# Last tile of a two-dimensional convolution: when its planes are built, which engine sums, and who issues its eight output writes

## The chip, the cores and the metric

The kernel runs on one core of one Trainium2 chip. The metric is the time of one execution on the device in microseconds (us); several executions were timed and the median is given. A separate execution was profiled; its trace gives the start and length of every instruction, and all times "at" some microsecond below are counted from the first instruction of that trace.

The engines go by the names of the profile: PE is TensorE (matrix products) and PEld its weight loads, DVE is VectorE, ACT is ScalarE, POOL is GpSimd, SP is SyncE, which here only issues DMAs. A small q (SPq, ACTq) means that only the sequencer of the engine is at work, as when it issues a DMA. PSUM is the memory that PE writes its products to, in eight banks; SBUF is the working memory.

## What is computed

```python
def reference(x, w):             # x: (1, 224, 224, 96) bf16, w: (7, 7, 96, 96) bf16
    wp = jnp.pad(w, ((0, H - K), (0, W - K), (0, 0), (0, 0)))
    Xf = rfft2(x.astype(f32), axes=(1, 2))
    Wf = rfft2(wp.astype(f32), axes=(0, 1))
    Yf = jnp.einsum('bhwi,hwio->bhwo', Xf, Wf)
    return irfft2(Yf, (H, W), axes=(1, 2)).astype(bf16)
```

This is a circular convolution of a 224 x 224 image of 96 channels with a 7 x 7 filter that maps 96 channels to 96.

## The kernel before

**Tiles and rounds.** The image is cut into 7 tiles of 32 columns (`t` = 0 to 6; the last is `TL`). The rows are cut into 8 blocks of 28 (`NJ` = 8, `B` = 28), and each block of rows, with its halo, is transformed along the rows into 17 points (`NS` = 17). Points 0 and 16 are real (`REAL`), the other 15 are complex. One pass over a point of a tile is a round, `b_round(t, s, ...)` at line 510. The columns are not transformed: they are convolved directly, with the even and the odd columns apart, by three sets of taps (`TAPS`, 4 + 4 + 3), and a complex product is made of three real ones (`part` 0, 1, 2).

**A round on PE.** Its stationary operands (the weights that PEld loads) are slices of 128 columns of the transformed image `xf` or of planes `J`, which are sums and differences of `xf`; its moving operand is the transformed filter `WF`, 96 columns wide. A complex round has 33 matrix products: 12 and 7 of them go to bank `b0`, the other 14 to bank `b1`. Between the two runs stands `mid()`, and after them `end()`: there other jobs are put in, in the last tile the inverse transforms of the tile before (`Gm` against `tt`, 384 columns wide).

**A round on the other engines.** ACT copies the shared products out of `b0` into `tt_` (times -0.5 where needed). DVE makes `u` from `b0` and `tt_`, with one `scalar_tensor_tensor`, and `v` from `b1` and `tt_`. Then `ysum` (line 601) adds `v` and `u` and writes bf16. POOL makes this sum, except in rounds with `ydve` true, in which DVE makes it. `tt_`, `u` and `v` have two buffers each. In a round with planes the sum on POOL waits for the last plane operation.

**Planes.** `jit(t, g)` (line 474) makes the planes of a group of three rounds (`JGB`, the last group has two: 15 and 16), with three DVE operations: all four differences in one, then a sum, then two sums. They are put in behind `v` of the first round of the group before (`plan`, line 859): in the last tile in rounds 0, 3, 6, 9 and 12. There `ydve` is true (line 876), so that in rounds 3, 6, 9 and 12 DVE makes the sum and then the planes.

**The last tile's end.** Other tiles write their results to DRAM and read them back in another order. The last one keeps them in SBUF: rounds 0 to 12 (`SA` = 13) in `YA`, rounds 13 to 16 in `YB`. DVE then turns blocks of 32 x 32: `turn_a(0)` to `turn_a(3)` make `TA` out of `YA` (in rounds 13, 14, 15 and 16), and `turn_b` makes `TB` out of `YB`, in two operations, once the sum of round 16 is there. Then come 16 output pieces `(j, h)`, `j` a block of rows and `h` half of the tile's columns. For each, `first` (line 892) makes one product of 384 columns with the matrix `GA` from `TA`; `second` (line 897) adds four products of 96 columns with `GB[b]` from `TB` in the same bank, and copies the bank into `yo`, by DVE and ACT in turn. Eight `first` are made ahead, while `TB` is awaited; each later one stands behind a `second`. `GA` and `GB` are parts of `GY`, five matrices of 112 columns.

**The writes.** After both halves of a block `j`, one DMA of 168 KB writes it to the output: SP issues `j` = 0, 2, 4, 6, POOL 1, 3, 5, and ACT 7:

```python
eng = SE if j == NJ - 1 else GE if j % 2 else DE          # line 915
eng.dma_start(out=out[0, j * B:(j + 1) * B, ...].rearrange("m (q w) c -> m q (w c)", q=4), in_=yo[0:MO, ...])
```

**Order.** Each engine runs its instructions in the order in which the program calls them (`_Ordered`, line 76); a waiting instruction holds all that stand behind it on its engine. All of them are recorded in that helper, so every line of the profile says L86, and one goes by the tiles' names.

Of the kernel before, what the change touches and what calls it, by code (L numbers as in the profile page):

```python
# [14 lines left out]
B = 28  # L15
# [19 lines left out]
SA = 13  # L35
NB4 = 4
YMAX = 3
YBUF = 4
JGB = ((0, 3), (3, 6), (6, 9), (9, 12), (12, 15), (15, 17))
LAG = 4  # L40
CQ = {2: (11, 0), 3: (11, 2), 4: (9, 5), 5: (6, 8), 6: (3, 8)}
SH2 = (0, 8, 13, 17)
MERGE = ()
NP2 = 0
WARM0 = 2
BIAS = 3000.0

# [6 lines left out]
def kernel(  # L54
# [60 lines left out]
        return r  # L115

    def evac(out_ap, in_ap, n):
        if tail[0]:
            return tail_evac(out_ap, in_ap, n)
        cv, ca = 180 + 1.0 * n, 160 + 0.85 * n  # L120
        if load["v"] + cv <= load["a"] + ca:
            load["v"] += cv
            return VE.tensor_copy(out=out_ap, in_=in_ap)
        load["a"] += ca
        return SE.copy(out=out_ap, in_=in_ap)

    def tail_evac(out_ap, in_ap, n):
        tail[0] += 1
        return VE.tensor_copy(out=out_ap, in_=in_ap) if tail[0] % 2 else SE.copy(out=out_ap, in_=in_ap)

    def dma(out_ap, in_ap):
        return DE.dma_start(out=out_ap, in_=in_ap)
# [341 lines left out]
    def jit(t, g):  # L474
# [24 lines left out]
            sub(Jb[:, 5:7, i0:i1], Jb[:, 0:4:2, i0:i1], Jb[:, 1:4:2, i0:i1], ALU.add, 2 * PP * (c1 - c0)),  # L499
        ]  # L500

    yf_cur = {}

    def pairs(ap):
# [5 lines left out]
    def b_round(t, s, mid, end, ydve=False, planes=()):  # L510
# [25 lines left out]
                TE.matmul(o, lhsT=pl[:, (HALO - k) * NJ:(HALO - k) * NJ + 128], rhs=wv,  # L536
                          start=(k == 0 and not add), stop=(k == len(tp) - 1 and not both and m != 2 or not add and not both and k == len(tp) - 1))
        b0, b1 = bank(), bank()
        merge = t < 2 and s in MERGE
        tt_ = tv_pool.tile([128, 4 * C], F32, name="tt_")  # L540
        if s in REAL:
            for part in range(2):
# [21 lines left out]
        else:  # L564
            v = tv_pool.tile([128, 2, 2, C], F32, name="v")
            if merge:
                conv(b0, 2 * C, 0, 0, both=True)
                conv(b0, 2 * C, 2, 0, add=True)
                conv(b0, 3 * C, 1, 0, add=True)
                conv(b0, 0, 0, 1)  # L570
                conv(b0, C, 0, 2)
                SE.mul(out=tt_[:], in_=b0[:, 0:4 * C], mul=-0.5)
                u, pr = tt_[:, 2 * C:4 * C].rearrange("p (m o) -> p m o", m=2), tt_[:, 0:2 * C]
            else:
                for part in range(3):
# [63 lines left out]
    xs = xf_bufs[(TL + 1) % 2].rearrange("c p r s w j -> c (p r s w j)")  # L639
    assert NA + 2 * NBL <= 4 * NS * POS * NJ and NA <= 2 * (XW + 32)  # L640
    YA = xn_all[:, 0:NA].rearrange("p (g s o) -> p g s o", s=SR, o=2)
    TA = xs[:, 0:NA].rearrange("p (g w j e) -> p w j g e", j=NJ, w=4, e=4)
    TB = xs[:, NA:NA + NBL].rearrange("p (g w j e) -> p w j g e", j=NJ, w=4, e=4)
    YB = xs[:, NA + NBL:NA + 2 * NBL].rearrange("p (g s o) -> p g s o", s=SRB, o=2)
# [16 lines left out]
    def g_parts():  # L661
        for q in range(4):
            dma(GX[q * SR:q * SR + 2 * SA, 0, q * B:q * B + B], G[0:2 * SA, 0:B])
            yield
        for q in range(4):
            for b in range(NB4):
                r = q * SR + b * SRB
                dma(GX[r:r + SRB, 1 + b, q * B:q * B + B], G[2 * SA:2 * NS, 0:B])
                yield
        for k in range(NB4 + 1):  # L670
            GE.tensor_copy(out=GY[:, k].rearrange("p (m q) -> p q m", q=4), in_=GX[:, k].rearrange("p (q m) -> p q m", q=4))
            yield

    yo_free = [J_bufs[2][0:4 * B, i * PXC * C:(i + 1) * PXC * C] for i in range(2)]
# [120 lines left out]
    for r in range(NS + LAG):  # L795
        if r == 0:
            add(0, 4, fj[1][1] + fj[2][1])
        for p in range(3):
            if r == (1, 3, 5)[p]:
                new_xf(1, SH2[p], SH2[p + 1])  # L800
                fj = f_jobs(1, p)
                if p == 2:
                    for jg in range(2):
                        fj[jg][-1] = then_load(fj[jg][-1], 2, jg)
                add(2 * r + 1, 2 * r + (5, 5, 4)[p], fj[0] + fj[1])
        for p in range(3):
            if r == SH2[p + 1] + 1 - (p == 2):
                new_xf(2, SH2[p], SH2[p + 1])
                fj = f_jobs(2, p)
                if p == 2:  # L810
                    for jg in range(2):
                        fj[jg][-1] = then_load(fj[jg][-1], 3, jg)
                add(2 * r, 2 * r + (8, 7, 5)[p], fj[0] + fj[1])
        if r == PGRP[-2][1] + 1:
            assert not any(q[2] for q in qs[:len(PGRP) - 1])
            wtmp_cm.__exit__(None, None, None)
            t_pool = ctx.enter_context(tc.tile_pool(name="tt", bufs=NTT, side="right"))
            t2_pool = ctx.enter_context(tc.tile_pool(name="tt2", bufs=1, side="right"))
            yo_pool = ctx.enter_context(tc.tile_pool(name="yo", bufs=2, side="right"))
            g_pool = ctx.enter_context(tc.tile_pool(name="gp", bufs=1, side="right"))  # L820
            GX = g_pool.tile([128, 1 + NB4, 4 * B], BF16, name="GX")
            GY = g_pool.tile([128, 1 + NB4, 4 * B], BF16, name="GY")
            GA, GB = GY[:, 0], GY[:, 1:]
            GE.memset(GX[:], 0.0)
        if r == NS + 3:
            queue_c(0)
        for t in range(2):
            s = r - LAG * t
            if not 0 <= s < NS:
                continue  # L830
# [12 lines left out]
    for t in range(2, NT):  # L843
        if t == TL:
            GE.memset(YA[:, :, 2 * SA:, :].rearrange("p g s o -> p g (s o)"), 0.0)
        else:
            scr_tiles[t] = dr_pool.tile([TW, NJ, NS, 4 * C], BF16, name="scr")
        qs = []
        if t + 1 < NT:
            add(4 if t == 2 else 0, 26, a_jobs(t + 1))  # L850
        nold, nnew = CQ[t]
        k1 = 2 * NS if t < TL else 2 * NS - 2
        k0 = 10 if t == 2 else 3
        km = k0 + -(-(k1 - k0) * nold // (nold + nnew))
        add(k0, km, cj[:nold])
        cn = c_jobs(t - 1)
        cj = cn[nnew:]
        add(km, k1, cn[:nnew])
        plan = {}
        for g, (s0, s1) in enumerate(JGB):  # L860
            if g + 1 < len(JGB) or t + 1 < NT:
                plan[s0 if g + 1 < len(JGB) else s0 - 1] = g
        for s in range(NS):
            now = ()
            if s in plan:
                g = plan[s]
# [12 lines left out]
    turn_b()  # L879
    load["v"] = 2 * BIAS + load["a"]  # L880
    for f in cj:
        f()
    tail[0] = 2
    assert not pend
    if NP2:
        for c in reversed(ps_cms):
# [3 lines left out]
    MO = 4 * B  # L890

    def first(j, h):
        pc = bank()[0:MO, 0:NC]
        TE.matmul(pc.rearrange("p (w g e) -> p w g e", w=2, e=4), lhsT=GA, rhs=TA[:, 2 * h:2 * h + 2, j], start=True, stop=False)
        return pc

    def second(j, h, pc, yo):
        po = pc.rearrange("p (w g b e) -> p b w g e", w=2, b=NB4, e=4)
        for b in range(NB4):
            TE.matmul(po[:, b], lhsT=GB[:, b], rhs=TB[:, 2 * h:2 * h + 2, j], start=False, stop=b == NB4 - 1)  # L900
        tail_evac(yo[0:MO, (j % 2) * 2 * NC + h * NC:(j % 2) * 2 * NC + (h + 1) * NC], pc, NC)
# [47 lines left out]
```

## Time and profile before

| | us |
|---|---|
| median of 3 executions | 265.87 |
| lowest, highest | 265.08, 266.1 |
| the profiled execution | 266.41 |
| its span, first to last instruction | 264.7 |
| PE busy | 252.5 (95% of the span) |
| DVE busy | 215.8 (82%) |
| ACT busy | 198.6 (75%) |
| POOL busy | 101.5 (38%) |
| mean granted TensorE clock | 0.993 |

The busy time of PE covers nearly all of the span, because a matrix product of 96 columns shows as 206 ns, while the next one starts 42 to 43 ns later: starts have to be compared, not lengths. The engines work at different things at the end of the span than in the rest of it, so that shares of the whole say little of a change to the last tile.

### The profile page before, as it was taken

To read this page: it belongs to the slowest core of one execution; us is meant where nothing else is said; L and a number is where in the kernel's file an instruction comes from. 1 tells how busy PE (TensorE), PEld (TensorE's weight loads), DVE (VectorE), ACT (ScalarE), POOL (GpSimd) and SP (SyncE) were. 2 spreads that over 40 slices of the span, in tenths; PEclk is the share of its full clock that TensorE was granted. 3 is DMA by queue.
4 is the path that set the end of the run, shared out by engine and by line. 5 is a ranking of instruction groups with operands and counts; after the bars stand their busy time and mean duration, and the time that the engine had idled before them with its cause. 6 is when DMAs were issued, how large, how long until landed. Compare 5 with 4: busy or idle time off the path is not lost.

```text
span 264.7 us, 12207 instructions
## 1 busy us (share of the span) xinstructions
PE 252.5 (95%) x5160; PEld 234.3 (89%) x5160; DVE 215.8 (82%) x459; ACT 198.6 (75%) x500; POOL 101.5 (38%) x166
## 2 busy tenths in 40 slices
PE   8799998999999999999999999999999999999981
PEld 3569898999999999998999998999999999999861
DVE  5729799898978979977888788777978889899981
ACT  5529997659795566898988869989798886666652
POOL 7781033345355553234123332543143222424420
PEclk9999999999999999999999999999999999999997
DMA  6766210451111299896979449597959753585135
GB/s 162 182 192 152 73 51 2 154 159 47 50 47 47 85 254 208 239 268 180 290 226 244 150 108 315 180 258 185 325 193 206 209 186 125 145 169 155 55 111 175
DMA packets 41416, 43.44 MB, mean 164 GB/s; under 512 B 30836, under 2 KB 33104, under 8 KB 41362
## 3 DMA queue, kind: packets, MB, share of 16 engines
q1 hardware_dynamic: 41044, 41.98, 56.6%
q8 instruction: 40, 0.66, 1.1%
q0 software_dynamic: 192, 0.52, 0.7%
q10 hardware_dynamic: 126, 0.17, 0.2%
q14 instruction: 14, 0.11, 0.1%
HBM read 22.09 MB, written 19.66 MB: 158 GB/s over the span
## 4 chain that ended last, share of the span: by engine, by line
PE 82%; ACT 5%; DVE 4%; issue 3%; DMA 3%; POOL 1%; SPq 1%; DVEq 0%; ACTq 0%
PE pb L86 82%; ACT WF L86 3%; DMA WF<-in_x_dram 3%; DVE WF L86 1%; ACT xf L86 1%; POOL yf L86 1%; DVE J L86 1%; DVE u L86 1%; DVE xf L86 1%; SPq L86 1%; DVE yf L86 0%; ACT tt L86 0%; DVE v L86 0%; ACT tt__676 L86 0%; ACT tt__2951 L86 0%
## 5 line engine op out<-in xcount | busy, mean ns | idle before, releaser
L86 PE MATMUL pb<-WF,J 96*128 96x96 bf16 x2821 | 162.6, 206 | 0.5 <-DVE WF L86 0.3
L86 PEld LDWEIGHTS <-J 96*128 96x128 bf16 x2821 | 137.9, 98 | 8.7 <-DVE u L86 1.5
L86 POOL TENSOR_TENSOR yf<-v,u 128x384 bf16<-128x384 f32 x70 | 69.1, 1001 | 129.5 <-issue 69.2
L86 ACT CAST xf<-pb 96x408 bf16<-96x408 f32 (+3 forms) x143 | 67.2, 487 | 10.3 <-PE pb L86 8.5
L86 PE MATMUL pb<-WF,xf 96*128 96x96 bf16 x952 | 60.2, 206 | 1.1 <-ACT xf L86 0.5
L86 DVE TENSOR_TENSOR J<-xf 96x1824 bf16<-96x1824 bf16 (+1 forms) x84 | 57.5, 724 | 0.1
L86 PEld LDWEIGHTS <-xf 96*128 96x128 bf16 x952 | 47.3, 98 | 1.9 <-issue 0.9
L86 PE MATMUL pb<-Fm,xn 118*128 118x136 bf16 (+3 forms) x640 | 45.5, 199 | 0.9 <-DVE u L86 0.8
L86 ACT CAST WF<-pb 96x480 bf16<-96x480 f32 (+1 forms) x59 | 29.0, 573 | 5.0 <-PE pb L86 5.0
L86 PE MATMUL pb<-tt,Gm 102*84 102x384 bf16 (+1 forms) x132 | 32.1, 326 | 0.0
L86 PEld LDWEIGHTS <-xn 118*128 118x128 bf16 x640 | 30.5, 97 | 1.2 <-issue 1.2
L86 ACT CAST yo<-pb 84x384 bf16<-84x384 f32 (+1 forms) x66 | 28.2, 484 | 2.9 <-PE pb L86 2.6
L86 ACT CAST J<-pb 84x384 bf16<-84x384 f32 (+1 forms) x65 | 28.0, 484 | 2.8 <-PE pb L86 2.8
L86 DVE TENSOR_TENSOR J<-J 96x912 bf16<-96x912 bf16 (+2 forms) x42 | 22.8, 542 | 0.0
L86 PE MATMUL pb<-wq 98*128 98x120 bf16 (+1 forms) x288 | 21.2, 225 | 0.0
L86 PEld LDWEIGHTS <-wq 98*128 98x128 bf16 x288 | 19.4, 148 | 0.2
L86 PE MATMUL pb<-wu 128*128 128x512 bf16 x43 | 11.8, 435 | 1.1 <-DVE ct L86 1.1
L86 DVE TENSOR_TENSOR yf<-v,u 128x384 bf16<-128x384 f32 x20 | 11.3, 567 | 0.7
L86 PEld LDWEIGHTS <-Gm 102*84 102x84 bf16 (+1 forms) x132 | 11.1, 117 | 0.8
L86 DVE CAST WF<-pb 96x480 bf16<-96x480 f32 (+1 forms) x13 | 7.5, 610 | 5.4 <-PE pb L86 5.2
L86 POOL TENSOR_TENSOR xn<-v,u 128x384 bf16<-128x384 f32 x8 | 7.2, 926 | 11.8 <-DVE v L86 11.8
L86 ACT COPY xf<-xf 96x816 bf16<-96x816 bf16 (+3 forms) x20 | 11.2, 621 | 0.0
(404 smaller groups left out, 254.3 us busy)
## 6 DMA issues: line engine op xcount, KB each, us to landing
scr<-yf SPq DMA_DIRECT2D x30, 288.0 KB
xn<-in_x_dram SPq DMA_DIRECT2D x12, 672.0 KB
tt<-scr SPq DMA_DIRECT2D x24, 336.0 KB
out_dram<-yo SPq DMA_DIRECT2D x12, 252.0 KB
out_dram<-J SPq DMA_DIRECT2D x12, 252.0 KB
tt<-scr SPq DMA_DIRECT2D x6, 288.0 KB
WF<-in_x_dram SPq DMA_DIRECT2D x2, 672.0 KB
scr<-yf SPq DMA_DIRECT2D x6, 192.0 KB
```

The costliest lines, as they stand in the source:

```text
L86: r = fn(*a, **k)
```

## The change

All of it concerns the last tile (`t == TL`), except that the matrices `GY` are set up with 16 further columns of zeros.

- The planes of rounds 15 and 16 are not made together in round 12 in a buffer `J`. `late_planes` makes them by themselves: those of round 16 in round 8 (one operation of 608 elements), those of round 15 in round 11 (608, 152 and 304 elements). They lie in free parts of the buffer `xf` of the other tile.
- The sums of rounds 3, 6, 9 and 12 go from DVE to POOL (`t != TL` in the last call).
- In rounds 14 and 15 the product that both halves of `u` share is written to both by PE, with a moving operand that repeats its 96 columns (192 wide, four products), and the other terms are added to it in PSUM. DVE's `u` falls away; ACT copies it out of PSUM, as a part of `tt_`, and POOL reads it there.
- `GY` has 128 columns, and `pc` all 128 rows; 112 are copied out.
- Six `first` are made ahead, not eight.
- Of the 16 copies DVE makes seven (numbers 1, 3, 5, 8, 10, 12, 14) and ACT nine, among them both of block 7.
- SP issues the writes of blocks 0, 2, 4, 5, 6, 7, POOL those of 1 and 3, ACT none.

```diff
+TAILV = (1, 3, 5, 8, 10, 12, 14)
-MERGE = ()
+MERGE = (14, 15)
+FI = 6
+LROUND = {8: 16, 11: 15}
...
     def tail_evac(out_ap, in_ap, n):
         tail[0] += 1
-        return VE.tensor_copy(out=out_ap, in_=in_ap) if tail[0] % 2 else SE.copy(out=out_ap, in_=in_ap)
+        return VE.tensor_copy(out=out_ap, in_=in_ap) if tail[0] in TAILV else SE.copy(out=out_ap, in_=in_ap)
...
+    def late_planes(s):
+        x0, x1 = (xf_tiles[TL][0:C, ph, :, s].rearrange("c r w j -> c r (w j)") for ph in range(2))
+        o = LATE[s]
+        Jb = jbuf[(TL, s)] = xs[0:C, o:o + 7 * PP].rearrange("c (k q) -> c k q", q=PP)
+        pd, rd, qd = x1.ap
+        dpl = bass.AP(x1.tensor, x1.offset - NJ, [pd, [NJ, 2], rd, qd])
+
+        def sub(o, a, b, op, n):
+            def f():
+                load["v"] += 170 + n * PP / 1.92
+                return VE.tensor_tensor(out=o, in0=a, in1=b, op=op)
+            return f
+        ops = [sub(Jb[:, 0:4].rearrange("c (k r) q -> c k r q", r=2), dpl, x0.unsqueeze(1).to_broadcast([C, 2, 2, PP]), ALU.subtract, 4)]
+        if s not in REAL:
+            ops += [sub(Jb[:, 4], x0[:, 0], x0[:, 1], ALU.add, 1), sub(Jb[:, 5:7], Jb[:, 0:4:2], Jb[:, 1:4:2], ALU.add, 2)]
+        return ops
...
-        merge = t < 2 and s in MERGE
+        merge = t == TL and s in MERGE
...
                 conv(b0, C, 0, 2)
-                SE.mul(out=tt_[:], in_=b0[:, 0:4 * C], mul=-0.5)
+                SE.mul(out=tt_[:, 2 * C:4 * C], in_=b0[:, 2 * C:4 * C], mul=-0.5)
+                SE.copy(out=tt_[:, 0:2 * C], in_=b0[:, 0:2 * C])
...
+    LATE = {NS - 2: NA * 3 // 4, NS - 1: NA + 2 * NBL}
...
-            GY = g_pool.tile([128, 1 + NB4, 4 * B], BF16, name="GY")
+            GY = g_pool.tile([128, 1 + NB4, 128], BF16, name="GY")
             GE.memset(GX[:], 0.0)
+            GE.memset(GY[:, :, 4 * B:], 0.0)
...
-            if g + 1 < len(JGB) or t + 1 < NT:
+            if g + 1 < len(JGB) - (t == TL) or t + 1 < NT:
...
+            if t == TL and s in LROUND:
+                now = late_planes(LROUND[s])
...
-            b_round(t, s, mid, fills(qs, 2 * s + 1), bool(now) and not (t == TL and s >= SA), now)
+            b_round(t, s, mid, fills(qs, 2 * s + 1), bool(now) and t != TL, now)
...
-    live = {k: first(*k) for k in order[:8]}
+    live = {k: first(*k) for k in order[:FI]}
...
-        if 8 <= k < len(order):
+        if FI <= k < len(order):
...
-            eng = SE if j == NJ - 1 else GE if j % 2 else DE
+            eng = GE if j in (1, 3) else DE
```

More of the change, by code (lines that the diff above doesn't have):

```diff
@@ L117, in evac @@
     def evac(out_ap, in_ap, n):
-        if tail[0]:
-            return tail_evac(out_ap, in_ap, n)
         cv, ca = 180 + 1.0 * n, 160 + 0.85 * n
@@ L641 @@
     YA = xn_all[:, 0:NA].rearrange("p (g s o) -> p g s o", s=SR, o=2)
+    LATE = {NS - 2: NA * 3 // 4, NS - 1: NA + 2 * NBL}
+    assert 7 * PP <= NA // 4 and NA + 2 * NBL + 7 * PP <= 4 * NS * POS * NJ
     TA = xs[:, 0:NA].rearrange("p (g w j e) -> p w j g e", j=NJ, w=4, e=4)
@@ L670, in g_parts @@
         for k in range(NB4 + 1):
-            GE.tensor_copy(out=GY[:, k].rearrange("p (m q) -> p q m", q=4), in_=GX[:, k].rearrange("p (q m) -> p q m", q=4))
+            GE.tensor_copy(out=GY[:, k, 0:4 * B].rearrange("p (m q) -> p q m", q=4), in_=GX[:, k].rearrange("p (q m) -> p q m", q=4))
             yield
@@ L882 @@
         f()
-    tail[0] = 2
+    tail[0] = 0
     assert not pend
@@ L892, in first @@
     def first(j, h):
-        pc = bank()[0:MO, 0:NC]
+        pc = bank()[:, 0:NC]
         TE.matmul(pc.rearrange("p (w g e) -> p w g e", w=2, e=4), lhsT=GA, rhs=TA[:, 2 * h:2 * h + 2, j], start=True, stop=False)
@@ L900, in second @@
             TE.matmul(po[:, b], lhsT=GB[:, b], rhs=TB[:, 2 * h:2 * h + 2, j], start=False, stop=b == NB4 - 1)
-        tail_evac(yo[0:MO, (j % 2) * 2 * NC + h * NC:(j % 2) * 2 * NC + (h + 1) * NC], pc, NC)
+        tail_evac(yo[0:MO, (j % 2) * 2 * NC + h * NC:(j % 2) * 2 * NC + (h + 1) * NC], pc[0:MO], NC)
     order = [(j, h) for j in range(NJ) for h in range(2)]
     warm(WARM0)
-    live = {k: first(*k) for k in order[:8]}
+    live = {k: first(*k) for k in order[:FI]}
     LF = 4
```

## The prediction

> **What bounds the kernel now.** I read first what followed what at the end, then the stages, then single rows. Over the whole span the page's chain of work is PE at 82%, and PE's starts show why nothing can be won before 250 us: in the last tile up to 251.36 us products of 96 columns start 42 to 43 ns apart, without a gap that an engine's wait explains. So DVE work saved in rounds 0 to 13 is worth nothing by itself. The chain of work, cut to 245 us and later (start, us, what):
>
> ```profile
> 244.99 5.84 PE pb L86 x112
> 250.83 1.82 DVE xf L86 x2
> ...
> 252.78 1.49 PE pb L86 x8
> ...
> 254.27 4.36 PE pb L86 x64
> 258.66 0.89 ACT tt L86 x2
> ```
>
> The rounds end, then two turns on DVE hold PE, then 8 `first`, the 64 products of `second`, two copies, and no instruction that computes for the last 5.1 us. The busy time by stage (us busy of each engine, then granted clock, share of the DMA engines, GB/s):
>
> ```profile
> 245.00:250.00 5.00, 5.00 (x106) 4.54 (x104) 4.97 (x11) 3.17 (x11) 1.89 (x3) 1.00 0.23 69
> 260.00:262.00 2.00, 0.00 (x0) 0.00 (x0) 0.00 (x0) 0.00 (x0) 0.00 (x0) 0.80 0.79 241
> ```
>
> DVE has 4.97 of 5 us of work while PE does its last rounds: it lags behind PE. At 260 to 262 us only the writes run, at 0.79 of the DMA engines. DVE's part in order of time:
>
> ```profile
> 250.12 0.32 DVE L86 SCALAR_TENSOR_TENSOR u<-pb,tt__7453 128x192 f32<-128x192 f32 x1
> 250.36 0.54 DVE L86 TENSOR_TENSOR v<-tt__7453,pb 128x384 f32<-128x384 f32 x1
> 250.82 1.82 DVE L86 STREAM_TRANSPOSE xf<-xn 128x768 f32<-128x768 f32 x2
> 252.56 0.51 DVE L86 TENSOR_TENSOR xf<-tt__7497,pb 128x384 bf16<-128x384 f32 x1
> 253.18 1.04 DVE L86 STREAM_TRANSPOSE xf<-xf 128x384 f32<-128x384 f32 x2
> ```
>
> These are `u` and `v` of round 15, `turn_a(2)` and `(3)`, the sum of round 16, `turn_b`: 3.86 us from the start of `v` to the end of `turn_b` at 254.22, nearly without a gap. PE's last product for this `v` started at 249.18 and takes 206 ns, so `v` could have begun at 249.43: it comes 0.93 us late.
>
> **Part 1: sums to POOL, planes ahead, no `u` in rounds 14 and 15.** DVE loses four sums (4 x 0.56 us), the planes in round 12 (0.78 + 0.23 + 0.31 us) and two `u` (0.32 each). It gains 0.46 us in round 8 (row `J<-J` 96x608, 461 ns) and 0.46 + 0.23 + 0.31 in round 11. Following DVE in the new order: planes of round 15 until 244.41, `u` and `v` of round 12 until 245.2, `v` of 13 until 246.87 (its product ends at 246.29), then `turn_a(0)`. That waits for POOL's sum of round 12: sums of 0.93 us, of which those of rounds 9 and 11 start behind planes (241.95 and 244.45), give 246.3, 0.57 us before DVE comes. `v` of 14 and `turn_a(1)` end at 249.32, and DVE stands free. `v` of 15 then begins with PE: the 0.93 us fall away, and PE's own delay is late next.
>
> That delay: eight products of 192 columns in place of 96. No row has this width; the bounds are the 42.5 ns pace of 96 columns (nothing) and the 162.5 ns of 384 (+0.96 us). I take 82.5 ns, in proportion: 8 x 40 = **+0.32 us** on PE. ACT's two copies (128x96 251 ns, 128x192 313 to 327) grow by 0.06 us and end at 249.75, just before. So `v` of 15 starts at 249.43 + 0.32 + 0.05 = 249.80, not 250.36: **-0.56 us**. From there DVE's 3.86 us stay, and `TB` is there at 253.66. `turn_a(3)` ends at 252.08; six `first` x 163 ns fit in before `TB`, so fewer of them cost nothing here. The new wait, ACT's `tt_` of round 16 for POOL's sum of round 14, ends at 249.4, before ACT comes (250.1). The 16 columns of zeros cost POOL some 0.1 us near the start (memset of 560 columns 555 ns), off the path.
>
> **Part 2: 128 columns.** PEld's rows from 245 us on, mean ns behind the busy time:
>
> ```profile
> L86 PEld LDWEIGHTS <-GY 128*112 128x112 bf16 x80 | 5.4, 131 | 2.3 <-POOL xf L86 1.5 <-issue 0.2
> L86 PEld LDWEIGHTS <-J 96*128 96x128 bf16 x78 | 3.6, 98 | 0.4 <-issue 0.3
> L86 PEld LDWEIGHTS <-Gm 102*84 102x84 bf16 x8 | 0.8, 118 | 0.2
> ```
>
> Loads of 128 columns are shorter than those of 112 and of 84, and the products' starts agree: 51 to 52 ns apart with `GY`, 42.5 ns with `J`. Bounds: no change, or J's pace; I take J's, since the row is the same load with the same 96 moving columns. The stage from the first to the last start of `second` was 4.55 us with 8 `first` within; now 64 x 42.5 ns and 10 x 162.5 ns less one step make 4.30: **-0.25 us**. The last product starts at 253.70 + 4.30 = 258.00 (was 258.82).
>
> **Part 3: copies and writes.**
>
> ```profile
> L86 SPq DMA_DIRECT2D out_dram<-tt x4: 801/840/925, 255.4 to 259.2; - x4
> L86 POOL DMA_DIRECT2D out_dram<-tt x3: 586/592/882, 256.4 to 258.9; - x3
> L86 ACTq DMA_DIRECT2D out_dram<-tt x1: 1437/1437/1437, 259.6 to 259.6; - x1
> ```
>
> Copies go on at 0.475 us (DVE) and 0.414 (ACT) from start to start. In the new order block 4 is copied at 257.30, block 7, both halves on ACT, at 259.05 (was 259.55). From block 4 on SP issues every write: four of 0.80 us with 0.12 between (that gap stood between the first two) end at 257.32 + 3.20 + 0.36 = **260.88 us**, against 261.02 for ACT's one. So 0.50 us that block 7 wins is spent in SP's queue, 1.03 us long at block 7.
>
> From the end of an issue to the last landing mark in the trace it took 1.89 us (block 0, alone), 2.65 (block 7) and 3.50 (block 6, among three queues). New writes come 0.92 us apart, and the packets of block 0 passed in 0.81, so they hardly meet: 2.1 us, near block 0. Last landing 260.88 + 2.1 = 262.98, against 263.67: **-0.7 us**. The 1.0 us after it stays.
>
> **The sum.** PE +0.32, DVE's lag -0.93 + 0.05, `second` -0.25, copies and SP's queue +0.67, landing -0.55: -0.69. The profiled execution (span 264.7, time 266.41) would be 265.7; it was 0.54 above the median, so the median goes from 265.87 to **265.2 us**.
>
> **The Trainium skill against it.** Its page "DMA: Bandwidth & Descriptors", section "Issuing engines are not separate DMA queues", says that all issuing engines share the same DMA engines and that issuing from several saves only the time to initiate, usually small. Here that time is not small (0.80 us beside 0.81 of packets); by the rule, rival A would be the result. Its page "SBUF — State Buffer", section "Who interferes with whom", says that a DVE instruction with two SBUF inputs and a POOL one that reads SBUF block each other. The rows agree:
>
> ```profile
> 220.43 1.00 POOL L86 TENSOR_TENSOR yf<-v,u 128x384 bf16<-128x384 f32 x1 [3.42 <-DVE v L86]
> 221.10 0.74 DVE L86 TENSOR_TENSOR yf<-v,u 128x384 bf16<-128x384 f32 x1
> ```
>
> The sum on DVE took 0.74 us beside POOL's, 0.56 alone. That is the mechanism of rival C.
>
> **Rivals.** *A, SP's queue costs nothing*: at the 356 ns median of SP's 24 `out_dram<-yo` block 7 goes out at 259.08; block 0 needed 2.81 us from issue to landing, which gives 261.89, while eight writes of 172 KB at 241 GB/s from 256.3 on give 262.4. The kernel would take 264.1 to 264.6, say 264.4. Against it: all four rows of this shape are 801 to 925.
>
> *B, slower: SP becomes the bound.* If each of its last four issues takes what ACT's took, 1.437 us, they end at 263.43, and with 2.1 us the last landing is 265.53: 267.7 us. It turns from gain to loss at (263.67 - 2.1 - 257.32 - 0.36) / 4 = 0.97 us an issue. For it: issues of SP stretch to 2.09 and 2.14 us in rows at 204 and 233 us, where the DMA engines are full. With 0.80 us an issue but block 6's 3.50 us to land it is 266.6.
>
> *C, slower: POOL comes late.* Beyond 1.21 us for each of its last two sums `turn_a(0)` waits; if planes hold them so that each takes double (1.85), it starts 1.28 us late, of which the 0.48 us of idle DVE before `v` of 15 hides a part: 266.0.
>
> *D, 128 columns change nothing*: `second` is 0.6 us longer, block 4 some 0.35 later: 265.5, within the forecast.
>
> **Chances.** 0.5% is 1.33 us, about what a measurement of this kernel can tell from no change. Forecast with D, 264.7 to 266.1: 0.69. A: 0.17. B: 0.09, of which a third up to 266.5. C: 0.05. Faster by over 0.5% (below 264.54) is A and a bit of the forecast: 0.19; slower (above 267.2) is half of B and a few rare things: 0.08; within: 0.73. The range takes in A, C and B's beginning: 264.2 to 266.5.
>
> **What would show it.** `LDWEIGHTS <-GY` at 98 ns and starts 42.5 ns apart; 192-wide products 82 ns apart; `v` of round 15 at 249.8 behind an idle DVE; first `second` at 253.7; four SP issues end to end from 257.3, the last ending near 260.9, and its landing 2 us later. The prediction is wrong if those four take other than 0.8 to 0.93 us, or if the last write lands later than 2.7 us behind its issue.

## The result, and the profile after

The changed kernel takes 264.34 us (median of 11 executions, 264.16 to 265.16); the kernel before, run beside it, 265.56 (11 executions, 265.03 to 266.18). The two medians differ by 1.22 us. The ratio on record is 0.9967, with a 95% interval from 0.9956 to 0.9977: 0.88 us faster, between 0.61 and 1.17. The prediction said 0.69 us.

**A measure for less than 0.5 us.** The profiled execution of the changed kernel took 265.16 us, with a span of 263.5. It is 1.2 us shorter than that of the kernel before, but not all of this is the change: PE's first products that need the second load of the image start at 9.83 us in the one trace and at 9.26 in the other, in code that is the same in both, and the 0.56 us stay until round 13. Executions of one kernel differ by such amounts. So in all that follows I also give times **from a mark**: the start of the first of two `pb<-tt,Gm` products (384 columns wide) that PE makes in round 13, at 245.05 us before and 244.49 after. From the mark to the end of the span, the *tail*, it is 19.65 us before and 18.98 after: **-0.67 us**, where the prediction's sum says -0.69.

The chain of work of the changed kernel, from 244 us on (start us, us, what):

```profile
243.96 4.36 PE pb L89 x79
...
248.64 0.55 ACT tt__7453 L89 x2
...
249.28 0.55 DVE v L89
...
250.65 1.39 DVE xf L89 x2
...
253.22 4.03 PE pb L89 x62
...
257.27 0.86 ACT tt L89 x2
```

The order is that of before. But DVE's part no longer begins with `xf` behind a PE that runs until 250.83: it begins with `v` of round 15, and ahead of it stand ACT and PE. What DVE did there:

```profile
247.82 0.97 DVE L89 STREAM_TRANSPOSE xf<-xn 128x768 f32<-128x768 f32 x1
249.28 0.55 DVE L89 TENSOR_TENSOR v<-tt__7453,pb 128x384 f32<-128x384 f32 x1 [0.49 <-ACT tt__7453 L89]
249.76 1.83 DVE L89 STREAM_TRANSPOSE xf<-xn 128x768 f32<-128x768 f32 x2
251.51 0.52 DVE L89 TENSOR_TENSOR xf<-tt__7495,pb 128x384 bf16<-128x384 f32 x1
252.13 1.04 DVE L89 STREAM_TRANSPOSE xf<-xf 128x384 f32<-128x384 f32 x2
```

Behind `turn_a(1)` DVE stands idle for 0.49 us and waits for ACT's `tt_`: it doesn't lag any more. From `v` to the end of `turn_b` it is 3.89 us (3.86 before). The stages by time (us busy of PE, PEld, DVE, ACT, POOL; then clock, share of the DMA engines, GB/s), PEld's loads of `GY`, and the issues of the writes:

```profile
245.00:250.00 5.00, 5.00 (x105) 4.89 (x106) 3.96 (x7) 3.19 (x10) 2.89 (x5) 1.00 0.24 68
260.00:262.00 2.00, 0.00 (x0) 0.00 (x0) 0.00 (x0) 0.00 (x0) 0.00 (x0) 0.75 0.71 224
```

```profile
L89 PEld LDWEIGHTS <-GY 128*128 128x128 bf16 x80 | 4.3, 96 | 2.3 <-issue 1.3
```

```profile
L89 SPq DMA_DIRECT2D out_dram<-tt x6: 801/802/925, 254.3 to 259.6; - x6
L89 POOL DMA_DIRECT2D out_dram<-tt x2: 589/734/879, 255.3 to 256.8; - x2
```

DVE has 3.96 us of work between 245 and 250 us, not 4.97. A load of `GY` takes 96 ns on the mean, not 131. None of SP's six issues is longer than 0.925 us. The whole way, in us from the mark:

| | before | after |
|---|---|---|
| `v` of round 15 starts | 5.31 | 4.80 |
| `turn_b` ends (`TB` is there) | 9.17 | 8.69 |
| last product of `second` starts | 13.78 | 13.06 |
| block 7 is copied | 14.50 | 14.03 |
| last issue of a write ends | 15.97 (ACT) | 15.93 (SP) |
| last landing mark | 18.62 | 18.02 |
| end of the span | 19.65 | 18.98 |

`TB` comes 0.48 us earlier and the last product of `second` 0.72; when block 7 is copied, 0.47 of it is left. The last issue gives nearly all of that back (0.04 left), and the landing, from the end of that issue on, is 0.56 shorter (2.09 us instead of 2.65).

### The profile page after: what moved, and what is told of

Its sections match the earlier page's. It is cut to its first block, busy times and chain, and to the rows that moved or that the text cites. A ratio compares the mean times of both kernels' runs of the same rounds, so it can differ in the third digit from the quotient of the medians.

```text
span 263.5 us, 12204 instructions
## 1 busy us (share of the span) xinstructions
PE 252.1 (96%) x5160; PEld 233.5 (89%) x5160; DVE 213.2 (81%) x453; ACT 198.9 (76%) x501; POOL 104.0 (39%) x170
## 4 chain that ended last, share of the span: by engine, by line
PE 81%; ACT 5%; DVE 4%; issue 3%; DMA 2%; POOL 1%; SPq 1%; ACTq 0%; DVEq 0%
PE pb L89 81%; ACT WF L89 3%; DMA WF<-in_x_dram 2%; DVE WF L89 1%; ACT xf L89 1%; DVE xf L89 1%; POOL yf L89 1%; DVE J L89 1%; DVE u L89 1%; SPq L89 1%; DVE v L89 0%; DVE yf L89 0%; ACT tt L89 0%; ACT tt__7453 L89 0%; ACT tt__676 L89 0%
## 5 line engine op out<-in xcount | busy, mean ns | idle before, releaser
L89 PE MATMUL pb<-WF,J 96*128 96x96 bf16 x2782 | 160.6, 206 | 0.4 <-DVE WF L89 0.3
L89 PEld LDWEIGHTS <-J 96*128 96x128 bf16 x2782 | 136.2, 98 | 8.6 <-DVE u L89 1.5
L89 PE MATMUL pb<-WF,xf 96*128 96x96 bf16 x991 | 61.9, 206 | 1.1 <-ACT xf L89 0.5
L89 DVE TENSOR_TENSOR J<-xf 96x1824 bf16<-96x1824 bf16 (+1 forms) x82 | 56.7, 731 | 0.1
L89 PEld LDWEIGHTS <-xf 96*128 96x128 bf16 x991 | 49.1, 98 | 2.0 <-issue 1.0
L89 POOL TENSOR_TENSOR xn<-v,u 128x384 bf16<-128x384 f32 x12 | 10.9, 923 | 9.3 <-DVE J L89 6.3
```

Source lines behind the costliest of these rows:

```text
L89: r = fn(*a, **k)
```

## The experiments

My theory was the prediction's: three parts, of which the first removes DVE's lag and pays for it on PE, the second shortens `second`, and the third gives back in SP's queue what it wins in the landing. Twelve kernels ran; their times stand together here, from the mark in us, and under "ratio" the time against the kernel before, run on the same chip.

| | `v` 15 | `TB` | last issue ends | last landing | tail | ratio (95%) |
|---|---|---|---|---|---|---|
| before | 5.31 | 9.17 | 15.97 | 18.62 | 19.65 | 1 |
| after | 4.80 | 8.69 | 15.93 | 18.02 | 18.98 | 0.9967 (0.9956 to 0.9977) |
| a_gy112 | 4.80 | 8.68 | 16.27 | 18.26 | 19.22 | 0.9980 (0.9968 to 0.9993) |
| a_nomerge | 4.66 | 8.53 | 15.78 | 17.80 | 18.76 | 0.9956 (0.9941 to 0.9971) |
| a_oldwrites | 4.80 | 8.69 | 15.50 | 18.52 | 19.56 | 0.9993 (0.9981 to 1.0006) |
| a_dvesums | 4.80 | 8.69 | 15.93 | 17.98 | 18.94 | 0.9982 (0.9969 to 0.9996) |
| a_planes12 | 4.80 | 8.69 | 15.94 | 18.06 | 19.02 | 0.9960 (0.9945 to 0.9975) |
| b_sums | 4.70 | 8.56 | 15.36 | 18.25 | 19.29 | 0.9966 (0.9950 to 0.9981) |
| n_pool5 | 4.66 | 8.53 | 15.13 | 17.84 | 18.87 | 0.9963 (0.9948 to 0.9978) |
| n_act7 | 4.66 | 8.54 | 15.35 | 18.20 | 19.23 | 0.9963 (0.9948 to 0.9979) |
| n_pool5_no13 | 4.66 | 8.53 | 15.13 | 17.31 | 18.33 | one execution |
| n_act7_no13 | 4.66 | 8.53 | 15.35 | 18.17 | 19.15 | one execution |
| n_half7 | 4.66 | 8.53 | 15.78 | 18.34 | 19.24 | 0.9951 (0.9932 to 0.9970) |
| n_pool15 | 4.66 | 8.54 | 15.30 | 17.70 | 18.66 | 0.9953 (0.9939 to 0.9967) |

The intervals of most ratios overlap. What follows is read from the tails: up to the last copy, steps that an edit leaves alone repeat there within 0.01 to 0.02 us.

The landing repeats less well, and each tail is that of one execution. The three kernels with the same writes and the same times of issue (after, a_dvesums, a_planes12) land at 18.02, 17.98 and 18.06. Of the eleven timed executions of n_act7 the shortest took 264.17 us, 0.47 less than the profiled one, whose mark, at 243.67 us, lies within 0.05 of the earliest of all fourteen traces (243.62). So some 0.4 us of that tail was missing in the shortest execution, unless its opening was shorter than in any trace. A difference in the landing of a few tenths that one trace shows need not be that of every execution.

### Part 1: what removed DVE's lag

**a_dvesums**: the sums of rounds 3, 6, 9 and 12 on DVE again.

```diff
-b_round(..., bool(now) and t != TL, now)
+b_round(..., (t == TL and s in (3, 6, 9, 12)) or bool(now) and t != TL, now)
```

> The changed kernel with the sums of rounds 3, 6, 9 and 12 of the last tile on DVE again, 4 x 0.56 us. Theory: until round 12 PE sets the pace and DVE has gaps, so the first three cost nothing; the sum of round 12 stands ahead of `turn_a(0)` and DVE has 0.17 + 0.49 us of gaps behind it up to `v` of round 15: 0.56 fits, `v` within 0.1 us of 249.28, tail 18.95 to 19.15. Rival (the sums on POOL are what took away DVE's lag of 0.93): `v` later by 0.4 to 0.6, tail 19.4 to 19.6.

The tail is 18.94: no cost behind the mark. `v` of round 13 came 0.60 us late (1.85 us from the mark instead of 1.25) and `v` of round 14 0.34 (3.21 instead of 2.87); DVE's row of `v` of round 15 shows where the rest went:

```profile
248.71 0.56 DVE L89 TENSOR_TENSOR v<-tt__7453,pb 128x384 f32<-128x384 f32 x1 [0.20 <-POOL xf L89]
```

The idle time ahead of it shrank from 0.49 to 0.20 us, and `v` came at the same 4.80. Ahead of the mark, from 231 us on, PE fell 0.17 us behind, compared with a_gy112, product by product, so that the sums may be worth 0.1 to 0.2 us there; one trace shows it, and the ratios (0.9982 and 0.9967, intervals that overlap) do not settle it.

**a_planes12**: the planes of rounds 15 and 16 in round 12 again.

```diff
-LROUND = {8: 16, 11: 15}
+LROUND = {}
-            if g + 1 < len(JGB) - (t == TL) or t + 1 < NT:
+            if g + 1 < len(JGB) or t + 1 < NT:
```

> The changed kernel with the planes of rounds 15 and 16 built in round 12 again. Times from the first `pb<-tt,Gm` product of round 13: `v` of round 15 at 4.80 in the changed kernel, behind 0.49 us of idle DVE, and 0.17 idle ahead of `v` of round 14. DVE has 1.32 us of planes in round 12 where it had 1.00 in round 11, and POOL's sum of round 12 comes later behind them. Theory: 0.3 to 0.7 us late at `turn_a(0)`, of which the gaps take up to 0.66: `v` at 4.80 to 4.95, tail 19.0 to 19.15. Rival (moving the planes is what removes the lag): `v` at 5.2 or later, tail 19.4.

```profile
248.44 0.55 DVE L89 TENSOR_TENSOR v<-tt__7452,pb 128x384 f32<-128x384 f32 x1 [0.48 <-ACT tt__7452 L89]
```

`v` at 4.80 behind 0.48 us of idle time: the place of the planes is worth nothing here. `turn_a(0)` began 0.25 us later (1.97 from the mark, 1.72 in the changed kernel), behind 0.16 us of waiting for POOL's sum of round 12, and the gap ahead of `v` of round 14 took this delay; the tail of 19.02 differs from 18.98 only in the landing.

**a_nomerge**: rounds 14 and 15 as before.

```diff
-MERGE = (14, 15)
+MERGE = ()
```

> The changed kernel with rounds 14 and 15 as before: the shared product in a bank of its own, DVE's `u` in both rounds, 96-wide products. Theory: PE wins back its 0.32 us and its last product for `v` of round 15 ends at 248.9 instead of 249.2, but DVE has two `u` of 0.32 us more, of which 0.17 us of idle time ahead of round 14's `v` and 0.49 ahead of round 15's can hide 0.66 in all: the two meet, `v` of round 15 starts within 0.15 us of the changed kernel's 249.28, tail 18.85 to 19.1. Rival 1 (the merge is a gain, DVE is the bound): `v` 0.3 to 0.6 us later, tail 19.3 to 19.6. Rival 2 (the merge is a loss of PE's 0.32): `v` at 249.0, tail 18.7.

```profile
246.95 0.97 DVE L89 STREAM_TRANSPOSE xf<-xn 128x768 f32<-128x768 f32 x1
248.00 0.36 DVE L89 SCALAR_TENSOR_TENSOR u<-pb,tt__7455 128x192 f32<-128x192 f32 x1
248.28 0.54 DVE L89 TENSOR_TENSOR v<-tt__7455,pb 128x384 f32<-128x384 f32 x1
248.74 1.83 DVE L89 STREAM_TRANSPOSE xf<-xn 128x768 f32<-128x768 f32 x2
```

`v` starts at 4.66, 0.14 us earlier than with the merged product, `TB` 0.16 and the end 0.22 earlier. `v` is still within what I had called a tie (0.15 us), the tail of 18.76 lies just beyond it (18.85), on the side of rival 2: `u` of round 15 can start at 4.38, 0.42 us ahead of the merged round's `v`, and holds `v` for 0.28 of it. By the traces the merged product is a **loss** within this change: 0.15 us up to the end of the last issue, and 0.07 more in the landing. The ratios (0.9956 and 0.9967) do not tell the two apart.

**b_sums**: the kernel before, with only the last tile's sums of rounds 3, 6, 9 and 12 moved to POOL.

```diff
-b_round(..., bool(now) and not (t == TL and s >= SA), now)
+b_round(..., bool(now) and t != TL, now)
```

> The kernel before with one part of the change alone: the sums of rounds 13 to 16's turn-over in the last tile, and all its others, on POOL; planes, matrices, product of rounds 14 and 15 and writes as before. Times from the first `pb<-tt,Gm` product of round 13: `v` of round 15 starts at 5.31 before, PE would allow it from 4.4 on. Theory: DVE's lag of 0.93 us ahead of that `v` goes with the 0.56 us of the sum of round 12, and what is left is at most 0.37: `v` between 4.4 and 4.75, tail 18.75 to 19.1 instead of 19.65. Rival (the lag comes from the planes and `u`, and the sum was paid in gaps): `v` at 5.1 or later, tail 19.45 or more. Since putting the sums back in the changed kernel cost nothing at that `v`, a gain here would mean that any one of the three parts is enough to remove the lag.

```profile
242.99 0.55 DVE L86 TENSOR_TENSOR v<-tt__7297,pb 128x384 f32<-128x384 f32 x1
...
245.65 0.98 DVE L86 STREAM_TRANSPOSE xf<-xn 128x768 f32<-128x768 f32 x1 [0.17 <-POOL xn L86]
...
248.38 0.54 DVE L86 TENSOR_TENSOR v<-tt__7453,pb 128x384 f32<-128x384 f32 x1
```

`v` of round 15 at 4.70, as the theory has it (4.4 to 4.75), and earlier than with all of part 1 (4.80): the four sums bring 0.61 us at `v`, the whole part 0.51. My theory put this down to the sum of round 12 alone; that is not shown. `v` of round 12, which stands ahead of that sum, already comes 0.70 us ahead of the mark (the first row), where it was 0.27 before, so the sums of the rounds before it count too. `turn_a(0)` (the second row) waits 0.17 us for POOL here. The tail is 19.29, later than 18.75 to 19.1, because block 7 landed 2.90 us behind its issue; that is the question of part 3. So with the sums on POOL the planes and the merged product have next to nothing left to win at `v` (4.66 without the merged product); and with the planes and the merged product, the sums have nothing left to win there (a_dvesums).

### Part 2: 128 columns

**a_gy112**: the matrices cut back to 112 columns.

```diff
-            GY = g_pool.tile([128, 1 + NB4, 128], BF16, name="GY")
+            GY = g_pool.tile([128, 1 + NB4, 4 * B], BF16, name="GY")
...
-        pc = bank()[:, 0:NC]
+        pc = bank()[0:MO, 0:NC]
```

> The changed kernel with the matrices of `second` cut back to 112 columns, all else as changed. I measure the tail from the first 384-wide `pb<-tt,Gm` product of round 13 to the end of the span: 19.65 us before, 18.98 in the changed kernel. My theory (the load of 128 columns sets the pace): `LDWEIGHTS <-GY` back at 131 ns, products 51 to 52 ns apart instead of 42 to 43, so that 64 products last 0.6 us longer; block 4, the first that SP's last queue waits for, is ready after 40 of the 64, 0.36 later, and the end comes 0.35 to 0.4 later: tail 19.35. Rival D (columns change nothing): tail 18.98 within 0.05. Third outcome: the whole 0.6 arrives, if block 7 and not SP's queue sets the end: 19.55.

The load's row, and PE from the first to the last product of `second`, with ten `first` between, here and then in the changed kernel:

```profile
L89 PEld LDWEIGHTS <-GY 128*112 128x112 bf16 x80 | 5.4, 131 | 1.8 <-issue 1.2
```

```profile
252.60 5.08 PE L89 MATMUL pb<-xf,GY 128*112 128x96 bf16 x74 [0.33 <-DVE xf L89]
```

```profile
253.22 4.52 PE L89 MATMUL pb<-xf,GY 128*128 128x96 bf16 x74 [0.35 <-DVE xf L89]
```

131 ns again, and 5.08 us for these 74 products, which take 4.52 with 128 columns: the 16 columns of zeros save 0.56 us on PE. Block 4 was issued 0.35 later and SP's last issue ended 0.35 later, as expected, but block 7 landed 1.98 us behind it, not 2.09, and the tail is 19.22: 0.24 us, so D is refuted, and somewhat over half of PE's gain is lost in SP's queue and in the landing.

### Part 3: who issues the writes

**a_oldwrites**: SP 0, 2, 4, 6, POOL 1, 3, 5, ACT 7.

```diff
-            eng = GE if j in (1, 3) else DE
+            eng = SE if j == NJ - 1 else GE if j % 2 else DE
```

> The changed kernel with the writes issued as before: SP blocks 0, 2, 4, 6, POOL 1, 3, 5, ACT 7. In the changed kernel block 7 is copied at 258.51 and its issue on SP ends at 260.41, 1.1 us of that behind blocks 4 to 6. Theory of the prediction (SP's queue gives back what the copies win, the landing is shorter): ACT issues block 7 from 258.55 to 259.99 (1.437 us), and it lands 2.65 us later, as before, near 262.64: tail within 0.2 us of 18.98, rather later. Rival 1 (six writes by SP are the gain): the end 0.55 us or more later, tail 19.5. Rival 2 (SP's queue is only a loss): landing 2.1 us behind an issue of 0.9 to 1.44 us, tail 18.0 to 18.6.

```profile
L89 SPq DMA_DIRECT2D out_dram<-tt x4: 801/835/930, 253.4 to 257.2; - x4
L89 POOL DMA_DIRECT2D out_dram<-tt x3: 586/592/882, 254.5 to 257.3; - x3
L89 ACTq DMA_DIRECT2D out_dram<-tt x1: 1437/1437/1437, 257.7 to 257.7; - x1
```

ACT's issue ends at 15.50, 0.43 us ahead of SP's last one in the changed kernel, and the tail is 19.56: 0.57 later. Rival 1 holds, and the times bear it out: the interval of the ratio, 0.9981 to 1.0006, does not meet that of the changed kernel (0.9956 to 0.9977). Block 7 lands 3.03 us behind its issue (2.65 before, 2.09 with six writes by SP). The last 2.5 us of the traffic, from 15.5 after the mark on (share of the DMA engines and GB/s at the end of each row):

```profile
259.16:259.66 0.50, 0.00 (x0) 0.00 (x0) 0.00 (x0) 0.00 (x0) 0.00 (x0) 1.00 0.91 194
259.66:260.16 0.50, 0.00 (x0) 0.00 (x0) 0.00 (x0) 0.00 (x0) 0.00 (x0) 1.00 0.87 267
260.16:260.66 0.50, 0.00 (x0) 0.00 (x0) 0.00 (x0) 0.00 (x0) 0.00 (x0) 0.86 0.83 280
260.66:261.16 0.50, 0.00 (x0) 0.00 (x0) 0.00 (x0) 0.00 (x0) 0.00 (x0) 0.50 0.47 169
261.16:261.66 0.50, 0.00 (x0) 0.00 (x0) 0.00 (x0) 0.00 (x0) 0.00 (x0) 0.50 0.12 43
```

and of the changed kernel, at the same distance from its mark:

```profile
259.99:260.49 0.50, 0.00 (x0) 0.00 (x0) 0.00 (x0) 0.00 (x0) 0.00 (x0) 1.00 0.71 234
260.49:260.99 0.50, 0.00 (x0) 0.00 (x0) 0.00 (x0) 0.00 (x0) 0.00 (x0) 1.00 0.83 246
260.99:261.49 0.50, 0.00 (x0) 0.00 (x0) 0.00 (x0) 0.00 (x0) 0.00 (x0) 0.51 0.75 230
261.49:261.99 0.50, 0.00 (x0) 0.00 (x0) 0.00 (x0) 0.00 (x0) 0.00 (x0) 0.50 0.58 191
261.99:262.49 0.50, 0.00 (x0) 0.00 (x0) 0.00 (x0) 0.00 (x0) 0.00 (x0) 0.50 0.02 6
```

With three queues the traffic runs out slowly: 169 and then 43 GB/s. With one it stays at 191 and then stops. What is late: many bytes ahead, POOL's block 5, or ACT's own write? The next two kernels split the old assignment; both start from a_nomerge.

**n_pool5**: block 5 by POOL, so that SP's queue is short. **n_act7**: block 7 by ACT.

```diff
-            eng = GE if j in (1, 3) else DE
+            eng = GE if j in (1, 3, 5) else DE                              # n_pool5
+            eng = SE if j == NJ - 1 else GE if j in (1, 3) else DE          # n_act7
```

> The kernel without the merged product (a_nomerge), and block 5 written by POOL, so that SP writes 0, 2, 4, 6, 7. Times from the first `pb<-tt,Gm` product of round 13: in a_nomerge SP's last issue ends at 15.78, the last landing is at 17.80, the end at 18.76. Theory 1 (the queue of issues on SP sets the end): block 7 is copied at 13.87, SP is free of block 6 by 14.25, so its issue ends near 15.15; with 2.0 to 2.1 us to land 17.2, tail 18.15. Theory 2 (the DMA engines are the bound, and several queues that write at once land late): the landing of block 7 comes 2.7 to 3.0 us behind its issue, tail 18.8 to 19.1. Between: eight writes at the 240 GB/s of the stage from the first packet on give a last packet near 17.1, tail 18.1 to 18.3.

> The kernel without the merged product (a_nomerge), and block 7 written by ACT, so that SP writes 0, 2, 4, 5, 6 and POOL 1 and 3: the half of the old assignment that n_pool5 leaves out. ACT's issue starts at 13.9 after the first `pb<-tt,Gm` product of round 13 and takes 1.437 us, until 15.34; SP's last, block 6, ends at 14.88. Theory 1 (what makes the landing of the old assignment 3.03 us long is block 5 among POOL's slower writes): it lands 2.1 us behind, 17.4, tail 18.4. Theory 2 (it is ACT's own write that lands late): 2.7 to 3.0 us behind, tail 19.0 to 19.3, later than the 18.76 of six writes by SP.

In n_pool5 SP's last issue ended at 15.13, 0.65 us earlier, exactly as theory 1 says, and the end came 0.10 us *later*: block 7 landed 2.71 us behind. In n_act7 the last landing came 2.85 us behind the end of ACT's issue, and the tail is 0.47 longer. It is not block 7's: ACT's write of block 7 landed 2.70 us behind its issue, at 18.05, and SP's block 6 at 18.20, 3.32 us behind its own (2.09 in a_nomerge). So a shorter queue on SP won nothing by itself in these two executions; either second queue beside SP's last writes made the landing later, by as much or more. The times do not tell either kernel from a_nomerge (both ratios 0.9963), and 0.10 us is hardly more than the landing's own scatter.

**n_pool5_no13** and **n_act7_no13**: the same two, without the writes of blocks 1 and 3.

```diff
+            if j not in (1, 3):
                 eng.dma_start(out=out[0, j * B:(j + 1) * B, ...], ...)
```

> n_pool5 with the writes of blocks 1 and 3 left out (those two parts of the output stay unwritten), so that a quarter of the bytes that stand ahead of block 7 in the DMA engines is gone, while SP's and POOL's issues of blocks 4 to 7 stay as they were. Times from the first `pb<-tt,Gm` product of round 13: in n_pool5 SP's last issue ends at 15.13 and block 7 lands 2.71 us later. Theory 1 (backlog: the DMA engines can't take the bytes as fast as they are issued): it lands 2.0 to 2.2 us behind, near 17.2, tail 18.2. Theory 2 (a write of POOL beside the last ones makes them slow, whatever is queued): still 2.6 to 2.8, tail 18.8.

> n_act7 with the writes of blocks 1 and 3 left out (those two parts of the output stay unwritten). In n_act7 ACT's issue of block 7 ends at 15.35 after the first `pb<-tt,Gm` product of round 13, and it lands 2.85 us later. Theory 1 (backlog): 2.0 to 2.2 us behind, near 17.45, tail 18.45. Theory 2 (a write that ACT issues lands late by itself): still 2.65 to 3.0, landing 18.0 to 18.3, tail 19.0 to 19.3.

They part, in one execution of each. With POOL beside SP, fewer bytes ahead bring the landing from 2.71 to 2.18 us, which fits backlog, theory 1. With ACT beside SP they bring next to nothing: the last landing is 2.82 us behind ACT's issue instead of 2.85, and block 7's own 2.64 instead of 2.70, although block 5 landed 1.94 us behind its issue there, so that no backlog stood ahead. That is near theory 2, but it is not ACT's write alone that is late: SP's block 6, issued from 14.08 to 14.88 beside ACT's, has its last landing mark at 18.17 after the mark, 3.29 us behind, and ACT's block 7 at 17.99. Block 6 shows the same in every trace in which ACT issued a write beside it: 3.21 to 3.97 us behind its issue in six traces (in three of them POOL issued block 5 as well), against 1.97 to 2.14 in the five in which SP issued blocks 4 to 7 alone. The traffic from 15.5 after the mark on, n_act7_no13 first, then a_nomerge:

```profile
259.99:260.49 0.50, 0.00 (x0) 0.00 (x0) 0.00 (x0) 0.00 (x0) 0.00 (x0) 1.00 0.57 132
260.49:260.99 0.50, 0.00 (x0) 0.00 (x0) 0.00 (x0) 0.00 (x0) 0.00 (x0) 1.00 0.83 221
260.99:261.49 0.50, 0.00 (x0) 0.00 (x0) 0.00 (x0) 0.00 (x0) 0.00 (x0) 0.56 0.61 163
261.49:261.99 0.50, 0.00 (x0) 0.00 (x0) 0.00 (x0) 0.00 (x0) 0.00 (x0) 0.50 0.42 151
```

```profile
259.12:259.62 0.50, 0.00 (x0) 0.00 (x0) 0.00 (x0) 0.00 (x0) 0.00 (x0) 1.00 0.72 218
259.62:260.12 0.50, 0.00 (x0) 0.00 (x0) 0.00 (x0) 0.00 (x0) 0.00 (x0) 1.00 0.73 240
260.12:260.62 0.50, 0.00 (x0) 0.00 (x0) 0.00 (x0) 0.00 (x0) 0.00 (x0) 1.00 0.75 194
260.62:261.12 0.50, 0.00 (x0) 0.00 (x0) 0.00 (x0) 0.00 (x0) 0.00 (x0) 0.69 0.43 151
```

With no backlog ahead the pair on two queues moves 132 to 221 GB/s, the single queue with all its backlog 194 to 240 until it runs out. Why two queues are slower than one is open: the trace doesn't say which DMA engine carried a packet.

**n_half7**: block 7 in two halves of 56 rows, by ACT and by SP, to use both queues for the last block.

```diff
+            for e_, r0, r1 in [(SE, 0, B // 2), (DE, B // 2, B)] if j == NJ - 1 else [(eng, 0, B)]:
+                e_.dma_start(out=out[0, j * B + r0:j * B + r1, ...], in_=yo[4 * r0:4 * r1, ...])
```

> a_nomerge with block 7's write cut in two by rows, 56 by ACT and 56 by SP, all else as in a_nomerge (SP's last issue ends there at 15.78 after the first `pb<-tt,Gm` product of round 13, block 7 lands at 17.80, tail 18.76). If an issue's time goes by its rows, ACT's half is issued from 13.9 to 14.6 and SP's from 14.97 to 15.37. Theory 1 (SP's queue sets the end): the last landing is 2.0 to 2.1 us behind 15.4, near 17.45, tail 18.4, 0.35 better. Theory 2 (the bytes ahead in the DMA engines set the end): 17.7 to 17.9, tail 18.7 to 18.9. Theory 3 (what ACT issues lands late): ACT's half lands 2.9 us or more behind its issue, tail 18.5 or later, depending on how long that issue is.

```profile
L89 SPq DMA_DIRECT2D out_dram<-tt x6: 801/802/931, 253.3 to 258.6; - x6
L89 ACTq DMA_DIRECT2D out_dram<-tt x1: 1433/1433/1433, 257.5 to 257.5; - x1
```

Half the rows take the same time to issue: 1.433 us on ACT (1.437 for 112 rows), and SP's last issue, of 56 rows, 0.802 (15.78 at its end, as with 112). My assumption that an issue goes by its rows was wrong. With nothing won in the queue, and ACT beside SP, the profiled execution has a tail of 19.24. The six timed ones reach from 264.02 to 264.65, and the profiled one is near the slow end of them, so its landing is not that of every execution; its ratio doesn't set it apart from a_nomerge.

**n_pool15**: blocks 1 and 5 by POOL, 3 by SP, to fill the DMA engines earlier and keep SP's queue short.

```diff
-            eng = GE if j in (1, 3) else DE
+            eng = GE if j in (1, 5) else DE
```

> a_nomerge with blocks 1 and 5 written by POOL and 3 by SP, so that SP writes 0, 2, 3, 4, 6, 7: the bytes of block 3 enter the DMA engines some 0.5 us earlier than by POOL, and SP's queue is free of block 4 when block 6 is ready. Times from the first `pb<-tt,Gm` product of round 13; a_nomerge: SP's last issue ends at 15.78, last landing 17.80, tail 18.76. By the durations of SP's issues (0.93, 0.88, then 0.80, 0.11 between) its last one ends near 15.25. Theory 1 (backlog of bytes, filled earlier, and one queue of POOL beside SP's last two): it lands 2.1 to 2.3 us behind, as in n_pool5_no13, 17.35 to 17.55, tail 18.35 to 18.5, the best of all. Theory 2 (a second queue beside SP's last writes slows them whatever came ahead): 2.6 to 2.8 behind, tail 18.85 to 19.0, no better than a_nomerge. The bytes alone, 1.38 MB at 240 GB/s from the first packet at 11.15, give 16.9 and so bound neither.

Between the theories: the issue ends at 15.30, block 7 lands 2.40 us behind, and the tail is 18.66, 0.10 better than a_nomerge, hardly more than the landing's scatter, and 0.32 better than the changed kernel. It is the shortest complete kernel by the trace; by the times (264.08 us, ratio 0.9953) it is faster than the kernel before, but it can't be told from a_nomerge (0.9956) or the changed kernel (0.9967).

## Why the prediction was right, and where it was not

**The time.** 265.2 was predicted and 264.34 measured. 0.31 of the 0.86 us lie in the base: the kernel before has a median of 265.56 in the eleven executions beside the new ones, and 265.87 in the three that the prediction started from. The rest lies in the step: it was forecast as -0.69, and is -1.22 by the two medians, -0.88 by the ratio (-0.61 to -1.17) and -0.67 by the tails of the two traces. These differ by no more than the openings of the executions do: the marks of the fourteen traces lie between 243.62 and 245.05 us. That the tails agree with the forecast within 0.02 us is in part luck: the landing was sized rightly for a reason that did not hold (below).

**PE's own delay, right in size, wrong as a price.** The products of 192 columns stand 82 to 85 ns apart (82.5 predicted), and PE is 0.32 us later. But "DVE's lag -0.93" and "PE +0.32" were booked as one bargain. The lag had three remedies in this change, and one of them, the four sums on POOL, takes away all but a third of it (b_sums, 0.61 us at `v`). These sums stand in rounds 3 to 12, so the prediction's sentence that DVE work saved in rounds 0 to 13 is worth nothing by itself does not hold. It added up what each edit takes off DVE without asking which of them were still needed; the merged product was not, and the tail of a_nomerge is 0.22 us shorter without it.

**`v`, DVE's 3.86 us, `turn_a(0)`.** 0.51 us won at `v` (0.56 predicted), 3.89 us from there to `TB`, 0.49 us of idle DVE (0.48). POOL's sum of round 12 was there when `turn_a(0)` came, at 246.20 directly behind `v` of round 13: rival C has no place in the changed kernel. Where the planes stand in round 12 and the sum is POOL's, its wait is there, 0.16 and 0.17 us long (a_planes12, b_sums).

**`second`.** From the first to the last start 4.32 us (4.30 predicted), at 42 to 43 ns a product, with loads of 96 ns on the mean. Rival D is refuted by its own row, and by a_gy112; its price was given as 0.3 us and is 0.24. But the prediction also said that six `first` instead of eight cost nothing. PE stood idle for 0.35 us ahead of the first `second` (its row is shown with a_gy112), about the time of two more at 163 ns, and these two now lie within the 4.32 us. From `TB` to the copy of block 7 it is 5.34 us, as before (5.33), and 5.83 in a_gy112, which has 112 columns like the kernel before. So what the shorter loads win there, the six `first` and the new division of the copies cost again; no run separates these two.

**SP's queue and the landing.** Four issues of 0.80 us with 0.11 between, ending 15.93 after the mark (15.83 predicted), and a landing 2.09 us behind (2.1). Both terms came out as sized, and with them rivals A (no cost) and B (1.437 us an issue) fell. (Rival A's second figure should be 262.0 instead of 262.4: eight times 172 KB at 241 GB/s take 5.7 us from 256.3 on. The forecast doesn't use it.) What the prediction had not seen is why the landing got shorter. It said that writes 0.92 us apart "hardly meet". They do meet: in the changed kernel block 4 landed 2.80 us and block 5 2.55 us behind their issues on SP, and only blocks 6 and 7 (2.14 and 2.09) come near block 0's 1.89, so that the 2.1 was partly luck. The runs show something narrower: with SP alone at the end the last write lands 1.98 to 2.12 us behind its issue (after, a_gy112, a_nomerge, a_dvesums, a_planes12), with ACT beside it 2.65 to 3.03 (block 7 in before, b_sums, a_oldwrites, n_act7), and with no backlog ahead still 2.64 (n_act7_no13). By the prediction's terms the old assignment would have made the changed kernel 0.19 us longer (ACT from 259.08 on, 1.44 us to issue, 2.65 to land: 263.17 instead of 262.98); it made it 0.57 longer (a_oldwrites). And SP's queue, which it gives as the price of the assignment, does not set the end alone: n_pool5 shortens it by 0.65 us, and the landing takes it all. Why a second queue makes the landing later stays open.

**The Trainium skill's rule.** Its page "DMA: Bandwidth & Descriptors", section "Issuing engines are not separate DMA queues", says that DMAs of all engines run on the same DMA engines and interleave, and that issuing from several saves only the time to initiate. n_pool5 and n_act7 agree with the first half: the issue ended 0.65 and 0.43 us earlier than in a_nomerge, and the end came later. They go beyond the second half: in these two traces the time of issue was saved, and the end still came 0.10 and 0.47 us later. The same page of the Trainium skill, in "Why a DMA increments its semaphore by 16 and not by 1", says that a DMA uses the largest number of engines, up to 16, that divides the slowest dimension on both sides. These writes have 28 and 112 there, which by the rule gives 14. The trace agrees for SP's writes: each leaves 14 completion packets of 4 bytes (84 for the six); each of POOL's leaves 16. By the rule two of 16 engines would then carry nothing of the last four blocks; the trace doesn't say which engine carried a packet, and no run here changed it.

## What to carry to other kernels

Where several edits each take work off the same late engine, its lag can be removed only once: work out after each edit what is left of it, and drop those that come after zero, above all one that pays on another engine. An output that ends a kernel has three ends in a row, the copy, the issue and the landing; shortening the first two helps only as far as the landing follows, and in the traces here a second queue beside the last writes made the landing later by as much as the issue was earlier, or more (the exceptions are n_pool15, by 0.10 us, and n_pool5_no13, which leaves two writes out). For steps of a few tenths of a microsecond, measure in the trace from a mark close ahead of the change, not from the start, and look at the times of the other executions before trusting what one trace shows of the landing.

## What the runs showed of the hardware

- The time to issue one of these writes did not depend on its rows: 0.80 us on SP (0.87 to 0.93 for its first two) and 1.43 to 1.44 on ACT, with 56 rows as with 112 (n_half7).
- Products of 96 columns stood 42 to 43 ns apart with stationary operands of 128 columns, and 74 products took 0.56 us more with 112: without its 16 columns of zeros the smaller matrix is the dearer one (a_gy112).
- Two writes of 172 KB, one from SP and one from ACT, issued within 0.17 us of each other with no backlog ahead, both landed late, 3.29 and 2.64 us behind their issues, where the four writes that SP issued before them took 1.87 to 1.94 (n_act7_no13, one execution).
